# Asking for input loads five casts ahead instead of eight, in cast order, and putting fetches and stores ahead of them

## The chip, the core and the metric

The kernel runs on one core of a Trainium2 chip. The core has a matrix engine (TensorE, "PE" in the profile, with weight loads shown as "PEld"), three engines for elementwise work (VectorE or DVE, ScalarE or ACT, GpSimd or POOL), and SyncE (SP), which in this kernel only issues DMA transfers. Each engine works through its own instructions in the order in which they were written; they wait for one another with semaphores. The metric is the device time of one execution in microseconds (us).

## The reference

Two computations stand one behind the other. First causal attention over 8 batches, 8 heads, 576 tokens and head size 64, in which 16 "beacon" keys and values stand ahead of the sequence and are never masked. Its output, read as 4608 tokens of width 512, then goes through a feed-forward layer that takes the maximum of three products:

```python
k_all = concatenate([beacon_k, k], axis=2); v_all = concatenate([beacon_v, v], axis=2)
scores = scale * q @ k_all.T          # causal mask on the part behind the beacons
a = softmax(scores)
x = (a @ v_all) -> [4608, 512]
h = maximum(maximum(x @ w1, x @ w2), x @ w3)      # [4608, 768]
out = h @ w_out                                    # [4608, 512], float32
```

## The kernel before, in words

**Units of work.** Attention is done in pairs of heads: four pairs a batch, 32 pairs in all, numbered 0 to 31 (pair 20 is the first of batch 5). One step of the main loop (`emit_all`) belongs to each pair p from 8 on. A step emits, in this order: the scores of pair p (`emit_burst`, matmuls at L495, exponentials at L513); on every second step, the product with v for the two pairs before (`emit_pv_whole`, L615); the causal masks (L535, GpSimd); and several units of the feed-forward layer (L691 the three first products, L739 the last), which lag the attention by about a batch and fill TensorE. Finished outputs are called y and are stored to DRAM by SP (L771).

**How q and k reach TensorE.** Inputs come as float32. `load_pair` (L225) has SP load q and k of a pair into a stage buffer, `cast_pair` (L260) has GpSimd turn them into bf16. TensorE needs them transposed. For batches 0 to 3 TensorE transposes them itself (L387). For batches 4 to 7 (pair 16 on; `B_PE = 4`) three DMA steps do it: `store_pair` (L372) writes the bf16 pair to a DRAM buffer, and `fetch_pair` (L379 for q, L380 for k) reads it back through a transposing DMA into `qT` and `kT`, of which there are four each. In the plan, the fetch of pair p is asked for in step p-3, the store in step p-4, the cast in step p-5 (for pairs 16 to 18 at the end of that step). `open_dram` (L363) puts a batch's beacon keys into its DRAM buffer, in the step of the batch's first store.

**How v gets there.** `load_v` (L284, L289) loads the v of a batch in two pieces, written v b.0 and v b.1 here, and `cast_v` (L305) has GpSimd turn them into bf16 in step 4b+1. The product with v in step 4b+2 reads them first.

**Stage buffers and the list of loads.** All these loads go into one pool of eight stage buffers (`st_pool`). From batch 2 on they stand in a list `loads`, and `next_load` takes the next from it. `C(fn)` makes a planned cast ask for one load right behind it. So the number of loads asked for ahead of their casts is set once, at the point in `second_batch` where `next_load` is called for several at once (L980); after it each cast asks for one. In the kernel before the list runs batch by batch: four pairs, v b.0, v b.1.

**The order on SP.** Everything named above, apart from the weights and a few first loads, is issued by SP, one after the other. What a step asks for is kept in `plan` under (step, 0), which is run after the second feed-forward unit, and (step, 1), which is run at the end; within an entry it stands in the order in which `at_step` was called. A DMA that has to wait holds all that stand behind it in SP's queue: a load waits until the cast has freed its buffer, a store for its cast, a fetch for its store and for the scores that last read the same `qT`, a y for its copy out of PSUM. SP's DMAs also share eight completion semaphores in turn, so each waits, besides, for the landing of the one eight places before it.

Of the kernel before, what the change touches and what calls it, by code (L numbers as in the profile page):

```python
# [17 lines left out]
def kernel(  # L18
# [15 lines left out]
    B, H, S, D = q.shape  # L34
# [26 lines left out]
    PPB = H // 2  # L61
    PPQ = PPB // n_quad
    NPAIR = B * PPB
    RING = 4

    B_PE = 4
# [34 lines left out]
    def head(g, j):  # L101
        return 4 * g + j

    def place(p):
        b, pi = divmod(p, PPB)
        return b, pi // PPQ, 2 * (pi % PPQ)
# [98 lines left out]
    by_pool = nc.gpsimd.tensor_copy  # L205
# [8 lines left out]
    def new_stage(key):  # L214
        stage[key] = st_pool.tile([128, STW], FP32, name="st")
        return stage[key]

    def load_pair(p, gate=None):
        b, g, j0 = place(p)
        hs = slice(head(g, j0), head(g, j0) + 2)  # L220
        st = new_stage(("pair", p))
        if gate:
            gate.memset(st[0:QP, 0:1], 0.0)
        for i, src in enumerate((q, k)):
            nc.sync.dma_start(  # L225
                out=st[0:QP, i * NQ2 : (i + 1) * NQ2].rearrange("p (h x) -> p h x", h=2),
                in_=src[b, hs].rearrange("h (p r) d -> p h (r d)", r=QR),
            )
# [28 lines left out]
    def cast_piece(p, i, cast):  # L257
        st = stage["pair", p]
        t16 = pair_pool.tile([QP, QR, 2, D], BF16, name=f"p16{i}")
        cast(  # L260
            t16.rearrange("p r h d -> p h r d"),
            st[0:QP, i * NQ2 : (i + 1) * NQ2].rearrange("p (h r d) -> p h r d", h=2, r=QR),
        )
        stage["pair16", p, i] = t16
# [8 lines left out]
    def load_v(b, piece, gate=None):  # L273
        st = new_stage(("v", b, piece))
        if gate:
            gate.memset(st[:, 0:1], 0.0)
        t_lo, t_hi = V_PIECES[piece]
        for t in range(t_lo, t_hi):
            i = t - t_lo
            dst = st[:, i * H * D : (i + 1) * H * D].rearrange("p (h d) -> p h d", h=H)  # L280
            lo = 0
            if t == 0:
                lo = Nb
                nc.sync.dma_start(  # L284
                    out=dst[0:Nb], in_=beacon_v[b].rearrange("h n d -> n h d")
                )
            t0 = k_tok[t] + lo
            n = k_rows[t] - lo
            nc.sync.dma_start(  # L289
                out=dst[lo : lo + n], in_=v[b, :, t0 : t0 + n, :].rearrange("h p d -> p h d")  # L290
            )

    def cast_v(b, piece, cast):
        st = stage.pop(("v", b, piece))
        if b not in v_tiles:
            v_tiles[b] = v_pool.tile([128, n_kt, H, D], BF16, name="v_sb")
        v_sb = v_tiles[b]
        t_lo, t_hi = V_PIECES[piece]
        t = t_lo
        while t < t_hi:  # L300
            t1 = t + 1
            while t1 < t_hi and k_rows[t1] == k_rows[t]:
                t1 += 1
            n = k_rows[t]
            cast(  # L305
                v_sb[0:n, t:t1].rearrange("p t h d -> p (t h d)"),
                st[0:n, (t - t_lo) * H * D : (t1 - t_lo) * H * D],
            )
            t = t1
# [19 lines left out]
    def load_w_out():  # L329
        nc.gpsimd.dma_start(  # L330
            out=w_out_sb, in_=moe_w_out.rearrange("(t p) m -> p t m", p=128)
        )

    def load_beacons(b0, b1, dst, queue=None):
        for b in range(b0, b1):
            (queue or nc.sync).dma_start(
                out=dst[Nb * (b - b0) : Nb * (b - b0 + 1)],
                in_=beacon_k[b].rearrange("h n d -> n h d"),
            )
# [87 lines left out]
    def place_beacons(p, copy):  # L427
        b, pi = divmod(p, PPB)
        copy(kTs[p % NT][:, 0:Nb], bT[:, pi, Nb * b : Nb * (b + 1)])
# [74 lines left out]
    def emit_burst(p):  # L504
        at[p] = at_pool.tile([128, AT_W], BF16, name="at_sb")
        for gi, first in enumerate(next_pairs()):
            off = 0
            for t, q0, q1 in groups(p)[gi]:
                for e in range(2):
                    score(p, t, e, q0, q1, acc[:, first + e, off : off + q1 - q0])  # L510
                off += q1 - q0
            for e0, e1 in ((0, 1), (1, 2)) if gi == 0 else ((0, 2),):
                nc.scalar.activation(  # L513
                    out=both_heads(p, gi)[:, e0:e1],
                    in_=acc[:, first + e0 : first + e1, 0 : g_width(p, gi)],
                    func=AF.Exp,
                    scale=scale,
                )
# [3 lines left out]
    def emit_masks(p, gi, dve=False):  # L522
        masked.add((p, gi))
        off = 0
        for t, q0, q1 in groups(p)[gi]:
            n = k_rows[t]
            lo, hi = max(q0, k_tok[t]), min(q1, k_tok[t] + n)
            if lo < hi:
                view = both_heads(p, gi)[0:n, :, off + lo - q0 : off + hi - q0]
                x0 = lo - k_tok[t]  # L530
                if dve:
                    m = tri[0:n, None, x0 : x0 + hi - lo]
                    nc.vector.tensor_mul(view, view, m.to_broadcast([n, 2, hi - lo]))
                else:
                    nc.gpsimd.affine_select(  # L535
                        out=view,
                        in_=view,
                        compare_op=ALU.is_ge,
                        fill=0.0,
                        base=x0,  # L540
                        pattern=[[0, 2], [1, hi - lo]],
                        channel_multiplier=-1,
                    )
            off += q1 - q0
# [264 lines left out]
    def at_step(p, g, *fns):  # L809
        plan.setdefault((p, g), []).extend(fns)  # L810

    def L(fn, *a):
        return lambda: fn(*a)

    def load_pairs(p0, p1):
        return [partial(load_pair, p) for p in range(p0, p1)]

    loads = []
    def load_first_v(b):
        if b == B_PE - 1:  # L820
            load_beacons(B_PE, B, bk32)
        load_v(b, 0)

    for b in range(2, B):
        loads += load_pairs(b * PPB, (b + 1) * PPB) + [L(load_first_v, b), L(load_v, b, 1)]

    def next_load(n=1, **gate):
        for _ in range(n):
            if loads:
                loads.pop(0)(**gate)  # L830

    def C(fn, *a):
        def run():
            fn(*a)
            next_load()

        return run
# [40 lines left out]
    def F(n=1, new_ps=ffn_psum.tile):  # L878
        for _ in range(n):
            assert emit_ffn(END, new_ps)  # L880
# [88 lines left out]
    def second_batch():  # L969
        for p in range(PPB, 2 * PPB):  # L970
            place_beacons(p + 1, by_act)
            emit_burst(p)
            for gi in range(NG):
                emit_masks(p, gi)
                if p < PPB + 2 and 0 < gi < 3:
                    cast_piece(p + 2, gi - 1, by_pool)
                if p == 2 * PPB - 1 and gi == 1:
                    cast_v(1, 1, by_pool)
                    next_load(gate=nc.gpsimd)
                    next_load(6)  # L980
            if p < PPB + 2:
                stage.pop(("pair", p + 2))
            if p == PPB + 2:
                load_w_out()
                cast_v(1, 0, by_pool)
            if p + 1 < 2 * PPB:
                turn_pair(p + 1, by_dve)
                F(2, next_psum)
        F(4, next_psum)
        for p in range(2 * PPB, 2 * PPB + 2):  # L990
            cast_pair(p, by_pool, by_pool)
            next_load()
        finish = emit_pv_whole(n_quad)
        turn_pair(2 * PPB, by_dve)
        F(2, next_psum)
        finish()

    for p in range(2 * PPB + 2, B_PE * PPB):
        at_step(p - 2, 0, C(cast_pair, p, by_pool, by_pool))
    for b in range(2, B):  # L1000
        p = b * PPB
        at_step(p + 1, 0, C(cast_v, b, 0, by_pool))
        at_step(p + 1, 1, C(cast_v, b, 1, by_pool))
    at_step(B_PE * PPB - 5, 1, L(by_pool, bk16, bk32))
    for b in range(B_PE, B):
        p = b * PPB
        at_step(p - 4, 0, L(open_dram, b))
        for i in range(PPB):
            at_step(p + i - 5, int(p + i < 19), C(cast_pair, p + i, by_pool, by_pool))
            at_step(p + i - 4, 0, L(store_pair, p + i))  # L1010
            at_step(p + i - 3, 0, L(fetch_pair, p + i))


    def emit_all():
# [76 lines left out]
```

## Time and profile before

| what | value |
|---|---|
| median of 3 runs | 288.83 us (286.57 to 289.18) |
| profiled execution | 288.73 us, its span 287.0 us |
| TensorE busy | 275.5 us, 96% of the span |
| VectorE, ScalarE, GpSimd busy | 175.0, 159.5, 137.1 us |
| DMA | 50.59 MB, mean 176 GB/s; SP's queue 68.8% of 16 engines' span |
| granted TensorE clock | 0.998 of full speed |

The span is the time from the first to the last instruction of the profiled execution; the 1.7 us between it and the execution's time lie around it. The profile's views used below are: busy time by engine; busy time by stage (windows); waits, each with what ended it; the chain of work that ended last, followed back from the end; and the timeline of one engine, whose rows give start, duration, engine, line and tiles ("SPq" is SP's queue: the duration is that of the issue, not of the transfer). In the list of DMA issues the last two numbers are KB each and the median us from issue to landing.

### The profile page before, as it was taken

Reading aid. Unit: us, or ns where it says so; the run is one execution under the profiler, and the core shown is the slowest. Engines: PE = TensorE matmul, PEld = TensorE weight load, DVE = VectorE, ACT = ScalarE, POOL = GpSimd, SP = SyncE. Lnnn points to the kernel's source line nnn. Section 1 sums busy time; section 2 is a strip of 40 time slices with the busy share of each in tenths; the row PEclk is TensorE's granted clock in tenths of the full one; section 3 lists DMA queues with packets and bytes.
Section 4 is the critical chain, followed back from the end, with each engine's and each line's share of the span. In section 5 each row is a group of like instructions: output and inputs, shape, how many; then the busy total and the mean of one; then the engine's idle time right before and its main releaser. Section 6 shows DMA issues by size and latency. Waiting matters only on the chain.

```text
span 287.0 us, 7607 instructions
## 1 busy us (share of the span) xinstructions
PE 275.5 (96%) x2996; PEld 156.7 (55%) x2996; DVE 175.0 (61%) x303; ACT 159.5 (56%) x299; POOL 137.1 (48%) x282
## 2 busy tenths in 40 slices
PE   7889899999999999999998999899999999999995
PEld 3457674566555555555555787455555554444442
DVE  3784765773856757464735383538363847875773
ACT  3697595886668566756674858566675640000000
POOL 7271889567359955475544846284336210000000
PEclk9999999999999999999999999999999999999999
DMA  8999999999999999978999999848452003004004
GB/s 147 193 185 222 232 218 203 263 203 254 245 259 259 242 291 227 171 194 210 305 216 205 224 302 247 169 114 247 109 140 108 2 2 116 30 1 148 0 0 146
DMA packets 85315, 50.59 MB, mean 176 GB/s; under 512 B 64416, under 2 KB 80032, under 8 KB 85280
## 3 DMA queue, kind: packets, MB, share of 16 engines
q1 hardware_dynamic: 80672, 45.76, 68.8%
q0 software_dynamic: 4048, 4.03, 9.0%
q8 instruction: 23, 0.38, 0.6%
q10 hardware_dynamic: 560, 0.33, 0.5%
q14 instruction: 12, 0.10, 0.1%
HBM read 35.13 MB, written 14.22 MB: 172 GB/s over the span
## 4 chain that ended last, share of the span: by engine, by line
PE 79%; DMA 12%; POOL 3%; DVE 2%; issue 1%; ACT 1%; SPq 1%; POOLq 0%
PE acc L691 44%; PE acc L739 15%; PE acc L615 10%; PE acc L495 7%; DMA st<-in_v_dram 4%; DMA st<-in_k_dram 3%; DMA kT<-k_dram 2%; DMA quad<-in_k_dram 2%; PE acc L387 1%; POOL v_sb L305 1%; POOL at_sb L535 1%; ACT at_sb L489 1%; SPq L225 1%; DVE kT L415 1%; PE acc L757 0%
## 5 line engine op out<-in xcount | busy, mean ns | idle before, releaser
L691 PE MATMUL acc<-xT,w_sb 128*128 128x512 bf16 (+4 forms) x744 | 135.3, 338 | 0.0
L709 DVE TENSOR_TENSOR hT<-hT,acc 128x512 bf16<-128x512 bf16 x102 | 70.0, 688 | 59.1 <-PE acc L691 49.7
L691 PEld LDWEIGHTS <-w_sb 128*128 128x128 bf16 x744 | 69.3, 98 | 59.6
L535 POOL TENSOR_SCALAR_AFFINE_SELECT at_sb<-at_sb 128x256 bf16<-128x256 bf16 (+2 forms) x176 | 62.8, 378 | 75.1 <-ACT at_sb L513 71.1
L513 ACT ACTIVATE at_sb<-acc 128x208 bf16<-128x208 f32 (+3 forms) x140 | 89.5, 737 | 8.8 <-PE acc L495 7.5
L260 POOL CAST p<-st 96x768 bf16<-96x768 f32 x56 | 45.2, 831 | 10.2 <-DMA st<-in_q_dram 9.2
L739 PE MATMUL acc<-w_out_sb,hT 128*128 128x512 bf16 (+2 forms) x246 | 48.4, 348 | 0.0
L746 DVE COPY y<-acc 128x512 f32<-128x512 f32 (+1 forms) x35 | 21.9, 628 | 22.2 <-PE acc L739 13.3
L739 PEld LDWEIGHTS <-hT 128*128 128x128 bf16 x246 | 22.7, 98 | 21.8 <-DVE hT L709 1.6
L711 ACT CAST hT<-acc 128x352 bf16<-128x352 f32 x18 | 8.1, 452 | 47.0 <-PE acc L691 47.0
L711 DVE CAST hT<-acc 128x512 bf16<-128x512 f32 (+1 forms) x48 | 26.6, 554 | 9.1 <-PE acc L691 8.9
L495 PE MATMUL acc<-qT,kT 64*128 64x208 bf16 (+1 forms) x336 | 26.8, 280 | 3.6 <-DMA kT<-k_dram 2.9
L764 ACT COPY y<-acc 128x320 f32<-128x320 f32 x1 | 0.4, 425 | 46.0 <-PE acc L757 46.0
L495 PEld LDWEIGHTS <-kT 64*128 64x128 bf16 x336 | 15.4, 94 | 16.0 <-DMA kT<-k_dram 3.3
L638 DVE TENSOR_TENSOR xT<-raw,recip 128x576 bf16<-128x576 f32 x28 | 23.7, 887 | 0.0
L615 PE MATMUL acc<-at_sb,v_sb 128*32 128x512 bf16 (+5 forms) x672 | 22.8, 281 | 0.0
L625 ACT COPY raw<-acc 128x512 f32<-128x512 f32 x28 | 15.8, 633 | 4.8 <-PE acc L615 4.3
L305 POOL CAST v_sb<-st 128x1536 bf16<-128x1536 f32 (+2 forms) x21 | 18.2, 894 | 0.0
L615 PEld LDWEIGHTS <-v_sb 128*32 128x32 bf16 (+1 forms) x672 | 14.6, 96 | 6.7
L489 ACT ACTIVATE at_sb<-acc 128x1024 bf16<-128x1024 f32 (+3 forms) x16 | 13.1, 859 | 3.9 <-PE acc L480 3.8
L615 PE MATMUL acc<-at_sb,ones 128*32 128x512 bf16 (+3 forms) x336 | 14.9, 284 | 0.0
L433 DVE COPY kT<-acc 128x576 bf16<-128x576 bf16 x12 | 9.0, 753 | 6.4 <-PE acc L387 6.4
(69 smaller groups left out, 171.2 us busy)
## 6 DMA issues: line engine op xcount, KB each, us to landing
out_dram<-y SPq DMA_DIRECT2D x35, 256.0 KB, 3.4
st<-in_q_dram SPq DMA_DIRECT2D x28, 288.0 KB, 6.0
st<-in_k_dram SPq DMA_DIRECT2D x28, 288.0 KB, 6.6
st<-in_v_dram SPq DMA_DIRECT2D x24, 256.0 KB, 7.0
w_sb<-in_moe_w_dram POOLq DMA_DIRECT2D x6, 384.0 KB, 7.2
q_dram<-p SPq DMA_DIRECT2D x16, 144.0 KB, 2.8
k_dram<-p SPq DMA_DIRECT2D x16, 144.0 KB, 2.4
st<-in_v_dram SPq DMA_DIRECT2D x8, 224.0 KB, 7.0
```

Of the source, the lines that this page charges most:

```text
L260: cast(t16.rearrange("p r h d -> p h r d"), st[0:QP, i * NQ2 : (i + 1) * NQ2].rearrange("p (h r d) -> p h r d", h=2, r=QR),)
L305: cast(v_sb[0:n, t:t1].rearrange("p t h d -> p (t h d)"), st[0:n, (t - t_lo) * H * D : (t1 - t_lo) * H * D],)
L495: nc.tensor.matmul(ps, kTs[p % NT][hs, 128 * t : 128 * t + 128], qTs[p % NT][hs, q0:q1], start=True, stop=True, tile_position=(64 * e, 0),)
L513: nc.scalar.activation(out=both_heads(p, gi)[:, e0:e1], in_=acc[:, first + e0 : first + e1, 0 : g_width(p, gi)], func=AF.Exp, scale=scale,)
L535: nc.gpsimd.affine_select(out=view, in_=view, compare_op=ALU.is_ge, fill=0.0, base=x0, pattern=[[0, 2], [1, hi - lo]], channel_multiplier=-1,)
L615: nc.tensor.matmul(acc[32 * j : 32 * j + 32, bank, lo + q0 - qa : lo + qb - qa], lhsT, at_view(PPQ * quad + j // 2, t, j % 2, q0, qb), sta ...
L638: nc.vector.tensor_mul(xT[:, 2 * g + i, c0 : c0 + S], raw[:, i], recip)
L691: nc.tensor.matmul(ps[:, a:b], w_in[i][:, ct, 128 * ft : 128 * (ft + 1)], xT[:, ct, x0 : x0 + b - a], start=(ct == 0), stop=(ct == n_ct - 1),)
L709: nc.vector.tensor_max(h[:, lo:hi], h[:, lo:hi], ps[:, lo:hi])
L711: (by_act if hi < TOKB else by_dve)(h[:, lo:hi], ps[:, lo:hi])
L739: nc.tensor.matmul(ps[:, lo:hi], hT[:, ft, 128 * tt : 128 * (tt + 1)], w_out_sb[:, ft, lo:hi], start=(ft == 0), stop=(ft == n_ft - 1),)
L746: (by_act if hi < d_model else by_dve)(y[:, lo:hi], ps[:, lo:hi])
```

## The change

The list `loads` is sorted by the step in which each load is cast, in place of batch by batch; `cast_step` and `v_step` give that step and are now used for the casts as well. The burst in `second_batch` asks for three loads, not six. The planned entries of `open_dram`, `fetch_pair` and `store_pair` are written ahead of the casts (and so of the loads that the casts ask for), not among them; the fetch of a step comes ahead of its store. The beacon keys of batches 4 to 7 are loaded with pair 16, not with v 3.0.

```diff
-    def load_pairs(p0, p1):
-        return [partial(load_pair, p) for p in range(p0, p1)]
-
-    loads = []
-    def load_first_v(b):
-        if b == B_PE - 1:
+    def cast_step(p):
+        return (p - 2, 0) if p < B_PE * PPB else (p - 5, int(p < 19))
+
+    def v_step(b, piece):
+        return (b * PPB + 1, piece)
+
+    def load_turned_pair(p, **gate):
+        if p == B_PE * PPB:
             load_beacons(B_PE, B, bk32)
-        load_v(b, 0)
-
-    for b in range(2, B):
-        loads += load_pairs(b * PPB, (b + 1) * PPB) + [L(load_first_v, b), L(load_v, b, 1)]
+        load_pair(p, **gate)
+
+    loads = [(cast_step(p), 2 * (p >= B_PE * PPB), partial(load_turned_pair, p)) for p in range(2 * PPB, NPAIR)]
+    loads += [(v_step(b, i), 1, partial(load_v, b, i)) for b in range(2, B) for i in range(2)]
+    loads = [load for _, _, load in sorted(loads, key=lambda x: x[:2])]
...
                     next_load(gate=nc.gpsimd)
-                    next_load(6)
+                    next_load(3)
...
+    for p in range(B_PE * PPB, NPAIR):
+        if p % PPB == 0:
+            at_step(p - 4, 0, L(open_dram, p // PPB))
+        at_step(p - 3, 0, L(fetch_pair, p))
+        at_step(p - 4, 0, L(store_pair, p))
     for p in range(2 * PPB + 2, B_PE * PPB):
-        at_step(p - 2, 0, C(cast_pair, p, by_pool, by_pool))
+        at_step(*cast_step(p), C(cast_pair, p, by_pool, by_pool))
     for b in range(2, B):
-        p = b * PPB
-        at_step(p + 1, 0, C(cast_v, b, 0, by_pool))
-        at_step(p + 1, 1, C(cast_v, b, 1, by_pool))
+        for i in range(2):
+            at_step(*v_step(b, i), C(cast_v, b, i, by_pool))
     at_step(B_PE * PPB - 5, 1, L(by_pool, bk16, bk32))
-    for b in range(B_PE, B):
-        p = b * PPB
-        at_step(p - 4, 0, L(open_dram, b))
-        for i in range(PPB):
-            at_step(p + i - 5, int(p + i < 19), C(cast_pair, p + i, by_pool, by_pool))
-            at_step(p + i - 4, 0, L(store_pair, p + i))
-            at_step(p + i - 3, 0, L(fetch_pair, p + i))
+    for p in range(B_PE * PPB, NPAIR):
+        at_step(*cast_step(p), C(cast_pair, p, by_pool, by_pool))
```

The order of the two built programs on SP around the fetches of pairs 20 and 21, and of the loads from pair 12 on ("y" is a store of an output):

```
SP before: load 26, fetch 20, store 21, load 27, y, load v6.0, fetch 21, store 22, load v6.1, fetch 22
SP after:  y, fetch 20, store 21, load 25, load v5.0, y, load 26, fetch 21, store 22, load v5.1, fetch 22

loads before: 12 13 14 15 v3.0 v3.1 16 17 18 19 v4.0 v4.1 20 21 22 23 v5.0 v5.1 24 25 26 27 v6.0 v6.1 28 29 30 31 v7.0 v7.1
loads after:  12 13 16 14 17 15 v3.0 v3.1 18 19 20 21 v4.0 22 v4.1 23 24 25 v5.0 26 v5.1 27 28 29 v6.0 30 v6.1 31 v7.0 v7.1
```

The loads ahead of these (pairs 8 to 11, v 2.0, v 2.1) stand in the same order in both. The other four engines have the same instructions in the same order in both programs.

## The prediction

> **What bounds the kernel now.** I read the page's busy times first, then busy time by stage, then the waits of TensorE, then the chain of work that ended last, and at the end SP's own queue around the places that the chain names.
>
> ```profile
> span 287.0 us, 7607 instructions
> ## 1 busy us (share of the span) xinstructions
> PE 275.5 (96%) x2996; PEld 156.7 (55%) x2996; DVE 175.0 (61%) x303; ACT 159.5 (56%) x299; POOL 137.1 (48%) x282
> ```
>
> TensorE is busy for 275.5 of 287.0 us, so 11.5 us is all that it ever sits idle. A reordering that gives TensorE no less work can only win from these. Where they lie, by stage:
>
> ```profile
> core 0: us, PE busy (x) PEld busy (x) DVE busy (x) ACT busy (x) POOL busy (x), PEclk, DMA share, GB/s
> 60.00:148.00 88.00, 88.00 (x974) 48.84 (x971) 53.83 (x83) 61.28 (x120) 56.19 (x112) 1.00 1.04 240
> 148.00:153.00 5.00, 3.24 (x30) 1.93 (x29) 2.56 (x5) 1.75 (x5) 0.65 (x2) 1.00 0.97 178
> 153.00:180.00 27.00, 27.00 (x357) 20.62 (x355) 14.09 (x23) 18.23 (x33) 17.11 (x35) 1.00 1.15 243
> 180.00:183.00 3.00, 1.88 (x23) 1.21 (x21) 2.29 (x4) 0.82 (x3) 0.00 (x0) 1.00 0.78 183
> 183.00:240.00 57.00, 57.00 (x591) 30.27 (x588) 31.44 (x50) 35.13 (x65) 23.79 (x52) 1.00 0.39 103
> ```
>
> The first number after the stage's length is TensorE's busy time. From 60 to 240 us it is full except twice: 5.00 - 3.24 = 1.76 us idle around 150 us, and 3.00 - 1.88 = 1.12 us around 182 us. The remaining 8.6 us lie before 60 us and after 240 us, where the change reorders nothing that TensorE waits for (below). The last two columns matter as well: in the two long stages the DMA share is 1.04 and 1.15, so the DMA engines are fully booked at some 240 GB/s, and only after 183 us does the share fall to 0.39. The granted clock is 1.00 in all of them, so nothing here is a clock effect. What TensorE waited for at the two places:
>
> ```profile
> PE acc L495 <- DMA kT<-k_dram: 2.9, 2, 1.8
> ```
>
> Both times the first score matmul of a pair (L495) waited for the transposed k that `fetch_pair` brings. The chain of work shows which pairs:
>
> ```profile
> 113.48 0.85 PE acc L495 x11
> ...
> 142.56 0.85 PE acc L495 x11
> ...
> 149.08 2.73 DMA kT<-k_dram
> 151.81 0.05 issue
> 151.86 0.88 PE acc L495 x12
> ...
> 173.60 0.85 PE acc L495 x11
> ...
> 177.87 4.36 DMA kT<-k_dram
> ```
>
> Each step starts with its pair's L495 matmuls. Counted back from the last pair, 113.48 is pair 16, 142.56 pair 20, 151.86 pair 21 and 173.60 pair 24; the DMA at 149.08 is fetch 21, the one at 177.87 fetch 25. They are the second pairs of batches 5 and 6. Batch 4, without a stall, takes 142.56 - 113.48 = 29.08 us, or 7.27 us a step; batch 5 takes 173.60 - 142.56 = 31.04 us, 1.96 us more, of which 1.76 us are the idle time and 0.20 us a slower restart. Fetch 21 landed at 149.08 + 2.73 = 151.81 us; TensorE stood ready 1.76 us before 151.86, at 150.10. It was **1.7 us late**. Fetch 25 landed at 177.87 + 4.36 = 182.23 us, 1.1 us late.
>
> Why were they late? SP's queue just ahead of fetch 21:
>
> ```profile
> 142.08 0.40 SPq L771 DMA_DIRECT2D out_dram<-y  x1
> 142.58 0.38 SPq L284 DMA_DIRECT2D st<-in_beacon_v_dram  x1
> 143.01 3.88 SPq L289 DMA_DIRECT2D st<-in_v_dram  x3
> 146.98 2.06 SPq L379 DMA_TRANSPOSE qT<-q_dram  x1
> 149.08 1.26 SPq L380 DMA_TRANSPOSE kT<-k_dram  x1
> ...
> 151.54 1.14 SPq L289 DMA_DIRECT2D st<-in_v_dram  x2
> ```
>
> SP issues strictly in order. The three v DMAs of v 6.0 hold it for 3.88 us, 1.29 us each, against 0.57 us each for the two at 151.54: SP is held back by transfers in flight. Fetch 21 is requested by the program in step 18, before pair 19's burst, but SP reaches it in step 20 (146.98 lies behind 142.56). SP lags the program by two steps, because loads that nobody needs yet stand ahead of the fetch. How early those loads are:
>
> ```profile
> 186.78 1.46 POOL L305 CAST v_sb<-st 128x1536 bf16<-128x1536 f32 x1
> 188.18 1.59 POOL L260 CAST p<-st 96x768 bf16<-96x768 f32 x2
> 189.72 1.17 POOL L305 CAST v_sb<-st 128x512 bf16<-128x512 f32 x2
> ```
>
> These are the casts of v 6.0, of pair 30 and of v 6.1. The load issued at 143.01, whose back-pressure delayed the fetch, is first read at 186.78, over 40 us later.
>
> **The change part by part.** Only SP's queue changes: in the two built programs TensorE, VectorE, ScalarE and GpSimd have the same instructions in the same order. No byte and no DMA is added or removed.
>
> *Fewer loads ahead (the burst of six becomes three, so every later load is asked for about three casts later).* By the two orders on SP's queue, the loads that stood ahead of fetch 21 and now stand behind it are pair 27, v 5.1 and v 6.0. Ahead of fetch 25 they are pair 31, v 6.1 and v 7.0, the same sizes:
>
> ```profile
> st<-in_q_dram SPq DMA_DIRECT2D x28, 288.0 KB, 6.0
> ...
> st<-in_v_dram SPq DMA_DIRECT2D x24, 256.0 KB, 7.0
> ...
> st<-in_v_dram SPq DMA_DIRECT2D x8, 224.0 KB, 7.0
> st<-in_v_dram SPq DMA_DIRECT2D x8, 160.0 KB, 4.8
> ```
>
> A pair is q and k, 2 x 288 KB; v b.1 is 256 + 160 KB; v b.0 is 224 + 2 x 256 KB (and a small beacon part). Together 576 + 416 + 736 = 1728 KB, 1.77 MB, which at the 240 GB/s of the stage is 7.4 us of the DMA engines. If the queue stays full, fetch 21 lands 7.4 us earlier, 5.7 us before it is needed, and fetch 25 6.3 us before. If the queue does not stay full, SP has caught up with the program, and the fetches are earlier still, up to their place in the program. So the saving at the two places is bounded below by nothing (the lag does not shrink) and above by the whole stall; less than a quarter of the 7.4 us (1.7) removes the larger one, so I take the whole: 1.96 us for batch 5 and 1.12 us for batch 6, **3.08 us**.
>
> *Fetch and store ahead of the loads of the same step.* Fetch 20 no longer stands behind the load that the first v cast of step 17 asks for. But the second v cast's load, and with it three loads in all (25, v 5.0, 26), now lie between fetch 20 and fetch 21, where two lay (27, v 6.0). That is one pair, 576 KB or 2.5 us, more between these two, and it is already in the count of 1728 KB, which compares all that is ahead. I cost it at nothing beyond that; were it uncovered it would take 2.5 of the 5.7 us of slack.
>
> *Order of casts.* Pairs 16 and 17 are now loaded ahead of 14 and 15, as they are cast. GpSimd has waits there, but TensorE is at 88.00 of 88.00 us from 60 to 148, so no gain shows: nothing.
>
> *Loads no longer wait for the cast just before.* With three buffers more free, a load from pair 18 on finds its buffer free, and the stores now carry the wait for their cast themselves. Behind a waiting store stand the loads and fetches of the same step; the cast it waits for is a step older, so I take nothing; the bound is the lag itself (a rival below).
>
> *Before 60 us* the order on SP's queue is the same up to pair 12, so the idle time there stays; after 240 us only stores are left.
>
> **The sum** against the profiled execution: 288.73 - 1.96 - 1.12 = 285.65 us. What is late next is nothing on SP: TensorE is then full from 60 to 240 us, so no further gain can follow. The profiled 288.73 us stands 0.1 us under the median of 288.83 us, so the forecast is 1.1% below it; 1%, or 2.9 us, is about what a measurement of this kernel can tell from no change.
>
> **The rivals.** *One stall stays.* Three loads still stand ahead of fetch 21 and of fetch 25, and if SP's back-pressure, not the amount of work, sets the delay, one of the two may still be late: 288.73 - 1.96 = 286.8 or 288.73 - 1.12 = 287.6 us. For it speaks the 3.88 us that one v load holds SP; against it that v 5.0 now has a pair's load between it and the fetch. *The change does not do what it says:* the DMA engines, at a share above 1, keep the same lag, and the time stays at 288.7 us. Against it: work that is moved behind a fetch cannot delay it in an in-order queue.
>
> *Slower: the v loads come too late.* v 6.0 and v 6.1 are asked for four steps later than now (with the casts of steps 21 and 22, not 17 and 18), 29.08 us. At SP's present lag v 6.0 would be issued at 143.01 + 29.08 = 172.1 us, its last part 3.9 us later, and land 7.0 us after that, at 183.0, 3.8 us before its cast at 186.78. v 6.1 would go out at 151.54 + 29.08 = 180.6, and land 1.1 + 4.8 us later, at 186.5, 3.2 us before its cast at 189.72. Behind that cast there is no slack at all:
>
> ```profile
> 190.79 1.54 PE L615 MATMUL acc<-at_sb,v_sb 128*32 128x512 bf16 x40
> ```
>
> TensorE reads v_sb from 190.79, while the cast ends at 189.72 + 1.17 = 190.89. So if SP's lag *grew* by more than 3.2 us, TensorE would wait one for one, at v 4.1, v 5.1 and v 6.1, and the fetches would be later too. A growth of 4.2 us gives 288.73 + 3 x 1.0 = 291.7 us. Against it speaks that the lag should shrink by 7.4 us. The Trainium skill has a rule on this side: "DMA: Bandwidth & Descriptors", Rules for kernel authors, says to issue a DMA early and wait for it late. Applied to the loads it would give this rival's 291.7 us; applied to the fetches it speaks for the forecast. The trace has the loads over 40 us early and the fetch late, so I weigh it for the fetch.
>
> **How the numbers follow.** Forecast, both stalls gone: 0.70, 285.65 us, by its own range 285.3 to 286.0 (0.35 us, the distance between the upper two of the runs shown, 288.83 and 289.18). One stall stays: 0.15, 286.8 to 287.6. Nothing moves: 0.06, 288.7. v late: 0.09, about 291.7. The likeliest case gives 285.6. A range of 285.0 to 287.6 takes in the first two cases, with a little below for runs that come lower by themselves (one run before took 286.57), and leaves 0.15 out. Faster by over 1% means under 285.9 us: most of the first case, 0.55. Its remainder, 0.15, with one stall and with nothing moved make 0.36 within 1%. Slower: 0.09.
>
> **What would show it.** Right: TensorE at 88.00, 5.00, 27.00, 3.00 busy in the stages above (shifted), no wait of L495 for kT, a batch of 29.1 us for batches 5 and 6, SP reaching fetch 21 well before pair 20's burst, and v casts starting where they do now. One stall: one L495 wait left. Wrong on the slow side: GpSimd's L305 waiting for st<-in_v_dram, and TensorE's L615 for v_sb. The forecast also fails if the fetches are early but the span loses time before 60 us, where I hold the order to be the same.

## The result, and the profile after

| what | before | after |
|---|---|---|
| median of the runs | 289.0 us (286.57 to 289.98, 6 runs) | 285.32 us (284.76 to 286.7, 6 runs) |
| profiled execution | 288.73 us, span 287.0 us | 285.18 us, span 283.5 us |
| ratio after / before | | 0.9894, 95% interval 0.9849 to 0.9938 |

The changed kernel is 1.1% faster; the forecast was 285.6 us. Medians and ranges are of all runs of a kernel, while a ratio leaves out the runs in a slower state, over 1.5% longer than the kernel's fastest, and so is not the quotient of the medians. On another chip the same kernel took 285.31 us against 289.66 us (the run `after_again` below). The busy times on the page of the changed kernel:

```profile
span 283.5 us, 7622 instructions
## 1 busy us (share of the span) xinstructions
PE 274.7 (97%) x2996; PEld 156.4 (55%) x2996; DVE 172.7 (61%) x303; ACT 159.4 (56%) x299; POOL 136.4 (48%) x282
```

TensorE does the same work in a shorter span: idle time went from 11.5 to 8.8 us. Busy time by stage, with the columns as before (length, TensorE busy, then the other engines, granted clock, DMA share, GB/s):

```profile
60.00:148.00 88.00, 88.00 (x969) 48.63 (x967) 53.14 (x82) 61.21 (x118) 56.38 (x113) 1.00 1.06 240
148.00:153.00 5.00, 5.00 (x38) 2.77 (x37) 3.04 (x5) 3.64 (x6) 1.65 (x4) 1.00 1.06 231
153.00:180.00 27.00, 27.00 (x370) 21.00 (x368) 15.14 (x25) 17.21 (x35) 16.33 (x33) 1.00 1.15 230
180.00:183.00 3.00, 3.00 (x15) 1.36 (x14) 1.82 (x3) 2.26 (x3) 2.09 (x6) 1.00 1.24 210
183.00:240.00 57.00, 57.00 (x586) 30.23 (x585) 33.53 (x54) 32.29 (x61) 22.04 (x47) 1.00 0.47 117
```

Both holes are gone: 5.00 of 5.00 us and 3.00 of 3.00 us, and TensorE is full from 60 to 240 us. The DMA engines are booked as before up to 180 us; the two short stages that had a share of 0.97 and 0.78 now have 1.06 and 1.24. The chain of work that ended last, at the same pairs:

```profile
112.91 0.85 PE acc L495 x11
...
141.99 0.85 PE acc L495 x11
...
149.53 0.83 PE acc L495 x12
...
171.22 0.85 PE acc L495 x11
...
178.78 0.83 PE acc L495 x12
...
200.32 0.85 PE acc L495 x11
```

No DMA stands between them any more. Batch 4 takes 141.99 - 112.91 = 29.08 us, as before; batch 5 takes 171.22 - 141.99 = 29.23 us (31.04 before) and batch 6 takes 200.32 - 171.22 = 29.10 us (203.86 - 173.60 = 30.26 before, by the same view). So 1.81 + 1.16 = 2.97 us of the 3.55 us between the profiled executions are the two stalls. The other 0.57 us were there already at pair 20 (142.56 against 141.99), and all of them at pair 9 (59.78 against 59.20). SP's queue is the same in both programs up to 64 us, so the change did not bring them. The start differs from run to run: pair 8's burst comes at 52.5 to 57.2 us in the profiled executions of the kernels below. Now SP's queue ahead of fetch 21 and fetch 25:

```profile
136.65 0.43 SPq L225 DMA_DIRECT2D st<-in_q_dram  x1
137.13 0.47 SPq L225 DMA_DIRECT2D st<-in_k_dram  x1
137.70 1.16 SPq L379 DMA_TRANSPOSE qT<-q_dram  x1
138.90 1.26 SPq L380 DMA_TRANSPOSE kT<-k_dram  x1
...
166.91 2.02 SPq L379 DMA_TRANSPOSE qT<-q_dram  x1
168.97 1.26 SPq L380 DMA_TRANSPOSE kT<-k_dram  x1
...
171.37 1.21 SPq L289 DMA_DIRECT2D st<-in_v_dram  x2
```

SP reaches k of fetch 21 at 138.90, 3.1 us ahead of pair 20's burst (141.99); before it was 6.5 us behind it (149.08 and 142.56). The two transfers landed at 142.88 and 173.53 us, 6.65 and 5.25 us before the bursts that read them (149.53, 178.78).

Below, the time by which a fetch is early is the start of the burst that reads it minus its landing; where TensorE waits, it is late by that wait. Landings are the last completion of the transfer in the trace, and KB ahead of a fetch are the sizes of the loads issued from 20 us on and before it, added up.

### The profile page after: what moved, and what is told of

It reads as the page before. It is cut to its first block, busy times and chain, and to the rows that moved or that the text cites. A ratio compares the mean times of both kernels' runs of the same rounds, so it can differ in the third digit from the quotient of the medians.

```text
span 283.5 us, 7622 instructions
## 1 busy us (share of the span) xinstructions
PE 274.7 (97%) x2996; PEld 156.4 (55%) x2996; DVE 172.7 (61%) x303; ACT 159.4 (56%) x299; POOL 136.4 (48%) x282
## 4 chain that ended last, share of the span: by engine, by line
PE 82%; DVE 1%; issue 0%
PE acc L691 46%; PE acc L739 16%; PE acc L615 11%; PE acc L495 7%; PE acc L387 2%; PE acc L757 0%; DVE hT L709 0%; DVE qT L422 0%; DVE y L764 0%; DVE kT L433 0%
## 5 line engine op out<-in xcount | busy, mean ns | idle before, releaser
L495 PE MATMUL acc<-qT,kT 64*128 64x208 bf16 (+1 forms) x336 | 26.9, 280 | 1.1 <-DVE hT L730 0.6
L495 PEld LDWEIGHTS <-kT 64*128 64x128 bf16 x336 | 15.5, 94 | 13.3 <-issue 2.6
L615 PE MATMUL acc<-at_sb,v_sb 128*32 128x512 bf16 (+5 forms) x672 | 22.8, 281 | 0.0
L638 DVE TENSOR_TENSOR xT<-raw,recip 128x576 bf16<-128x576 f32 x28 | 21.8, 821 | 0.0
L615 PEld LDWEIGHTS <-v_sb 128*32 128x32 bf16 (+1 forms) x672 | 14.5, 96 | 6.7
L615 PE MATMUL acc<-at_sb,ones 128*32 128x512 bf16 (+3 forms) x336 | 14.9, 284 | 0.0
```

Source lines behind the costliest of these rows:

```text
L495: nc.tensor.matmul(ps, kTs[p % NT][hs, 128 * t : 128 * t + 128], qTs[p % NT][hs, q0:q1], start=True, stop=True, tile_position=(64 * e, 0),)
L615: nc.tensor.matmul(acc[32 * j : 32 * j + 32, bank, lo + q0 - qa : lo + qb - qa], lhsT, at_view(PPQ * quad + j // 2, t, j % 2, q0, qb), sta ...
L638: nc.vector.tensor_mul(xT[:, 2 * g + i, c0 : c0 + S], raw[:, i], recip)
```

## The experiments

Theory: SP's queue carries loads that nobody needs yet, and the fetches stand behind them; a smaller lead is the whole gain. Rivals: the order of the list, or the place of the fetches in the plan, brings it; or it is not SP's order but the bytes in flight. The table holds the readings that the sections below use.

| kernel | lead | list | fetches | ratio to before, 95% interval | wait of L495 for kT | fetch 25 |
|---|---|---|---|---|---|---|
| before | 8 | by batch | among casts | 1 | 2.9 us | 1.1 late |
| after | 5 | by cast | ahead | 0.9894 (0.9849 to 0.9938) | 0 | 5.25 early |
| after_again | 5 | by cast | ahead | 0.9849 (0.9799 to 0.9899) | 0 | 3.9 early |
| e2 | 5 | by batch | among casts | 0.9859 (0.9810 to 0.9908) | 0 | 2.4 early |
| e3 | 5 | by cast | among casts | 0.9834 (0.9783 to 0.9884) | 0 | 4.6 early |
| e13 | 8 | by cast | among casts | 1.0100 (1.0054 to 1.0147) | 6.3 us | 3.3 late |
| e5 | 8 | by batch | ahead | 1.0115 (1.0045 to 1.0185) | 5.5 us | 3.2 late |
| e1 | 8 | by cast | ahead | 1.0101 (1.0057 to 1.0145) | 4.2 us | 4.2 late |
| e8 | 7 | by cast | ahead | 0.9891 (0.9814 to 0.9969) | 2.2 us | 2.2 late |
| e10 | 6 | by cast | ahead | 0.9877 (0.9805 to 0.9949) | 0 | 0.75 early |
| e9 | 3 | by cast | ahead | 0.9887 (0.9826 to 0.9947) | 0 | 7.2 early |
| e4 | 2 | by cast | ahead | 1.0878 (1.0794 to 1.0962) | 0 | 16.4 early |
| e11, late v left out | 8 | by batch | among casts | 0.9898 (0.9851 to 0.9944) | 0 | 13.6 early |
| e12, late v from GpSimd | 8 | by batch | among casts | 1.0171 (1.0107 to 1.0235) | 5.5 us | 3.6 early |

### The change with the old lead (e1)

The changed kernel, with eight loads ahead.

```diff
-                    next_load(3)
+                    next_load(6)
```

> The changed kernel with the burst at six again (eight loads ahead); cast order and fetches ahead of the loads stay. Theory (work that stands ahead of a fetch on SP decides): 20320 KB of loads stand ahead of fetch 21 (20512 before, 18752 changed) and 24000 ahead of fetch 25 (24000 before, 22240 changed), so both waits of L495 for kT come back, about 0.9 us at pair 21 and 1.1 us at pair 25: 287.0 to 287.8 us. Rival (the new order, not the lead, removes the stalls): no wait for kT, 285.3 us.

Measured: 293.21 us (292.04 to 296.08, 10 runs) against 290.98 us, 1.0% slower than before. The waits of TensorE, and SP's queue ahead of fetch 25:

```profile
PE acc L495 <- DMA kT<-k_dram: 4.2, 1, 4.2
```

```profile
172.54 0.46 SPq L225 DMA_DIRECT2D st<-in_q_dram  x1
...
174.51 5.80 SPq L289 DMA_DIRECT2D st<-in_v_dram  x3
180.41 2.75 SPq L379 DMA_TRANSPOSE qT<-q_dram  x1
183.20 1.27 SPq L380 DMA_TRANSPOSE kT<-k_dram  x1
```

v 7.0 holds SP for 5.80 us, and k of fetch 25 goes out at 183.20, 14.2 us later than at a lead of five (168.97), though TensorE starts pair 24 only 3.8 us later (174.99 against 171.22). Fetch 21 was 2.2 us early, fetch 25 4.2 us late, where waits of 0.9 and 1.1 us had been expected. Without the smaller lead nothing of the gain is left. That it is *slower* than before, outside the 287.0 to 287.8 us expected, is more than a missing gain: the next runs take the edits apart.

### The smaller lead alone (e2)

The kernel before, with five loads ahead.

```diff
-                    next_load(6)
+                    next_load(3)
```

> The kernel before with the burst at three (five loads ahead); list batch by batch, fetches and stores among the loads as before. Theory: 18592 KB of loads ahead of fetch 21, 160 KB less than in the changed kernel, so no wait for kT in batches 5 and 6; but pair 16 is then asked for only one cast ahead of its own and pair 17 two, so GpSimd waits some 5 us for pair 16 near 80 us; where masks come late by that, TensorE loses between nothing and 3 us: 285.3 to 288.5 us, with any loss before 110 us. Rival (order, not lead): both waits for kT stay, 288.7 us.

Measured: 286.23 us (285.61 to 287.77) against 290.98 us. By stage:

```profile
148.00:153.00 5.00, 5.00 (x39) 2.76 (x37) 3.14 (x6) 3.58 (x7) 2.17 (x4) 1.00 0.78 197
153.00:180.00 27.00, 27.00 (x366) 20.93 (x366) 14.68 (x25) 17.22 (x34) 16.25 (x33) 1.00 1.02 221
180.00:183.00 3.00, 3.00 (x21) 1.42 (x18) 1.88 (x3) 2.92 (x5) 1.66 (x4) 1.00 0.72 159
```

Both holes close with one number changed. The order of the list and of the plan is not needed for the gain. It may add slack that TensorE has no use for: fetch 25 was 2.4 us early here, with 22,080 KB ahead of it, and 5.25 and 3.9 us early in the two profiles of the changed kernel, with 22,240 KB. The loss before 110 us that was held possible did not come.

### The two orders, one at a time, at both leads (e3, e5, e13)

e3 is the changed kernel with its fetches and stores among the casts, as before; e13 is e3 with a lead of eight; e5 is the kernel before with its fetches and stores ahead of the casts. The edit of e3:

```diff
-    for p in range(B_PE * PPB, NPAIR):
-        if p % PPB == 0:
-            at_step(p - 4, 0, L(open_dram, p // PPB))
-        at_step(p - 3, 0, L(fetch_pair, p))
-        at_step(p - 4, 0, L(store_pair, p))
...
-    for p in range(B_PE * PPB, NPAIR):
-        at_step(*cast_step(p), C(cast_pair, p, by_pool, by_pool))
+    for b in range(B_PE, B):
+        p = b * PPB
+        at_step(p - 4, 0, L(open_dram, b))
+        for i in range(PPB):
+            at_step(p + i - 5, int(p + i < 19), C(cast_pair, p + i, by_pool, by_pool))
+            at_step(p + i - 4, 0, L(store_pair, p + i))
+            at_step(p + i - 3, 0, L(fetch_pair, p + i))
```

> The changed kernel with the plan's fetches and stores among the casts again; list and lead of the change stay. Theory: the loads ahead of fetch 21 and fetch 25 are the same as in the changed kernel (18752 and 22240 KB), so no wait for kT and 285.3 us. Rival (it matters that a step's fetch stands ahead of the step's loads): 286.5 to 288 us with at least one wait for kT.

> The kernel before with the plan's fetches and stores ahead of the casts and their loads, nothing else: list batch by batch, eight ahead. Theory: loads ahead of fetch 21 and fetch 25 are as before (20512 and 24000 KB), both waits for kT stay, 288.7 us. Rival (fetches ahead of the loads of their step are the cure): 285.3 us.

> The changed kernel with the burst back at six (lead of eight) and with the planned fetches and stores among the casts as before: of the three edits only the order of the loads is left. With fetches and stores ahead of the loads and the sorted order, lead eight was 1.0% slower than before; fetches and stores ahead alone (batchwise order) 1.2% slower. If the plan's order is what harms at lead eight, this kernel stands at the kernel before, ratio 0.995 to 1.005, with fetch 25 about 1 us late. If the cast order harms too, it is at 1.005 to 1.01, with a wait of L495 for kT of over 2 us. If the cast order were a gain of its own, it would be under 0.995.

Measured: e3 285.75 us (284.77 to 287.31) and e5 295.2 us (291.83 to 296.75) against 290.98 us; e13 291.1 us (289.6 to 294.46, 10 runs) against 289.0 us. The waits of TensorE for kT, of e5 and of e13:

```profile
PE acc L495 <- DMA kT<-k_dram: 5.5, 2, 3.2
```

```profile
PE acc L495 <- DMA kT<-k_dram: 6.3, 4, 3.3
```

At a lead of five the plan's order makes no difference that can be seen (e3 and after). At a lead of eight either order alone is 1.0 to 1.2% slower than before, and so are both together. In e5 the first wait is for fetch 17: it landed 7.08 us after pair 16's burst before (120.56, 113.48), 0.5 us early, and 9.76 us after it here (122.47, 112.71), 2.2 us late. That is 2.7 us more. What stands ahead of fetch 17 in all is the same in both, 17,024 KB; but in e5 the loads of three pairs and v 5.0 stand between fetch 16 and fetch 17, before it was those of one pair and v 5.0, and v 5.0 held SP for 6.96 us, before for 4.86. Why two pairs' loads moved from ahead of fetch 16 to behind it delay fetch 17 is not shown. At a lead of five no delay of this kind reaches TensorE. Why each order costs about as much as both together stays open too: the KB asked for ahead of fetch 25 are the same 24,000 in e1, e5, e13 and before, so a count of all that stands ahead doesn't tell these four apart. The profiled executions of e1 and e13 (295.96 and 294.46 us) lie above the medians of their kernels, so a usual run may have shorter waits than these (in e1's, 3.4 us of the distance to before are there at pair 8 already, 57.15 against 53.74); that they are slower than before is read from the ratios.

### Leads between and below (e8, e10, e9)

The changed kernel with leads of seven, six and three.

```diff
-                    next_load(3)
+                    next_load(5)   # e8; next_load(4) in e10, next_load(1) in e9
```

> The changed kernel with the burst at five (seven loads ahead). Theory (KB of loads ahead of the fetch): 23232 KB ahead of fetch 25, between 22240 in the changed kernel, where it landed 5.25 us early, and 24000 with eight ahead, where it came 4.2 us late; in proportion it lands at about the time it is needed: a wait of 0 to 1 us, 285.5 to 287 us, no drop of the clock. Rival (only the eighth load, whose buffer is freed by the cast just before it, holds SP): fetch 25 is over 3 us early as in the changed kernel, 285.3 us.

> The changed kernel with the burst at four (six loads ahead). Theory: 22656 KB ahead of fetch 25, in proportion 3 us early, no wait for kT, 285.3 us like the changed kernel. Rival (the lead of five is special): over 287 us.

> The changed kernel with the burst at one (three loads ahead). The prediction's slower mechanism by itself: v 6.1 stands behind store 28 on SP, some 183 us, and lands some 2 us after the 186.2 us at which its cast starts in the changed kernel; likewise v 4.1 and v 5.1. GpSimd's L305 waits for st<-in_v_dram and TensorE for v_sb, one for one, about 2 us a batch: 288 to 292 us, fetches all early. Rival (loads have slack at three too): 285.3 us.

Measured, against 289.66 us: e8 287.13 us (285.41 to 290.38), e10 286.02 us (284.46 to 288.08), e9 286.21 us (285.15 to 286.84). Fetch 25 goes from 4.2 us late at a lead of eight to 2.2 late, 0.75 early, 5.25 early (3.9 in the second run) and 7.2 early at seven, six, five and three, and the wait ends between seven and six. This is the theory's own dose, in its direction but not in proportion to the KB: e8's wait is 2.2 us where 0 to 1 was expected, e10's slack 0.75 us where 3 was. The rival of e8, that only the eighth load holds SP, falls, since fetch 25 is late with seven. Below six a smaller lead gives fetches more slack and TensorE nothing, since it is full already. At three the v loads have used theirs up; the casts of v 6.1 on GpSimd in the changed kernel and in e9:

```profile
186.16 1.17 POOL L305 CAST v_sb<-st 128x512 bf16<-128x512 f32 x2
```

```profile
186.23 1.26 POOL L305 CAST v_sb<-st 128x512 bf16<-128x512 f32 x2
```

The 0.09 us more are a wait inside the group: v 6.1 landed at 186.82 us, between the two casts. In the changed kernel it landed at 177.55, 8.6 us before. The 288 to 292 us expected of e9 did not come: with less standing ahead of them, the v loads come just in time.

### One load less still (e4)

The changed kernel with a lead of two.

```diff
-                    next_load(3)
+                    next_load(0)
```

> The changed kernel with a lead of two: no burst, each cast asks for one load. This looks for the turning point of the slower rival. Lead three had v 6.1 landing just as its cast waited for it, with no time lost to speak of. Theory (one load less ahead puts each second v piece 7 us or so later than its cast can bear): GpSimd's L305 waits for st<-in_v_dram, TensorE's L615 waits for v_sb one for one, some us in each of batches 4 to 7, and after a long enough wait a lower granted clock: 295 us or more, GpSimd waits of 5 us and over. Rival (a smaller lead only shifts SP's queue, and the v loads stay in time because less stands ahead of them): 285 to 288 us.

Measured: 314.49 us (313.1 to 315.88, 2 runs) against 289.0 us. TensorE's and GpSimd's waits, and GpSimd's casts of v 6.1:

```profile
PE acc L615 <- POOL v_sb L305: 17.8, 10, 4.2
```

```profile
POOL v_sb L305 <- DMA st<-in_v_dram: 22.7, 11, 5.5
```

```profile
213.97 0.61 POOL L305 CAST v_sb<-st 128x512 bf16<-128x512 f32 x1 [4.54 <-DMA st<-in_v_dram]
215.03 0.61 POOL L305 CAST v_sb<-st 80x512 bf16<-80x512 f32 x1 [0.45 <-DMA st<-in_v_dram]
```

This is the slower rival of the prediction, by the waits that it named: GpSimd waits for v, and TensorE's L615 for GpSimd. They come at v 4.1, v 5.1 and v 6.1, as it said, and at v 2.1 and v 3.1 too. Its turning point lies between a lead of three and of two.

### Without the late v loads (e11)

The kernel before, lead of eight, with v of batches 4 to 7 neither loaded nor cast; the v of batch 3 stands in for it, so the outputs of these batches are not the reference's.

```diff
-        loads += load_pairs(b * PPB, (b + 1) * PPB) + [L(load_first_v, b), L(load_v, b, 1)]
+        loads += load_pairs(b * PPB, (b + 1) * PPB)
+        if b < B_PE:
+            loads += [L(load_first_v, b), L(load_v, b, 1)]
+        else:
+            loads += [lambda: None] * 2
...
+        if b < B_PE:
+            at_step(p + 1, 0, C(cast_v, b, 0, by_pool))
+            at_step(p + 1, 1, C(cast_v, b, 1, by_pool))
+        else:
+            at_step(p + 1, 0, next_load, lambda b=b: v_tiles.update({b: v_tiles[B_PE - 1]}))
+            at_step(p + 1, 1, next_load)
```

> The kernel before, lead of eight, but the loads and casts of v of batches 4 to 7 are left out, and the v of batch 3 is used in their place; every other DMA keeps its place on SP. So this kernel moves 4 x 1152 KB less. Theory (fetches 21 and 25 are late because SP's queue ahead of them is filled with early loads): without 5.1 and 6.0 ahead of fetch 21, and 6.1 and 7.0 ahead of fetch 25, both land in time; no L495 wait for kT from 60 to 240 us, 285.3 to 286 us on the terms of the profiled run of before (a ratio of 0.985 to 0.99). Rival (the transposing DMAs are slow by themselves, or the four qT and kT buffers set the time): the two waits stay at 1.76 and 1.12 us, ratio 1.00.

Measured: 285.72 us (285.68 to 287.44) against 289.0 us, a ratio of 0.9898 (0.9851 to 0.9944). By stage:

```profile
148.00:153.00 5.00, 5.00 (x38) 2.76 (x37) 3.14 (x6) 3.58 (x7) 2.17 (x4) 1.00 1.01 295
153.00:180.00 27.00, 26.95 (x366) 20.95 (x366) 14.68 (x25) 17.22 (x34) 13.80 (x30) 1.00 0.70 160
```

There is no wait for kT. Fetch 21 landed at 138.08 and fetch 25 at 165.81 us, 12.1 and 13.6 us before their bursts. Of the transposing DMAs and their buffers nothing was touched, so they are not the limit; the loads ahead of them are. Leaving these loads out frees their place on SP's queue and the DMA engines alike (the share from 153 to 180 us is 0.70, before 1.15); the next run tries to part the two.

### The v loads on another queue (e12)

The kernel before, with v of batches 4 to 7 issued by GpSimd.

```diff
+        queue = nc.gpsimd if b >= 4 else nc.sync
...
-                nc.sync.dma_start(
+                queue.dma_start(
```

> The kernel before, lead of eight, but the v loads of batches 4 to 7 are issued by GpSimd, not by SP, at the same place of the program; the same bytes move, as early as before. Theory A (the order and the hold on SP's queue delay the fetch: a v load of three DMAs held SP for 3.88 us): SP reaches fetch 21 several us earlier, no L495 wait for kT, a ratio of 0.985 to 0.99, if GpSimd's own casts don't come late from the issuing. Theory B (the bytes in flight on the DMA engines, booked over 1.0 from 153 to 180 us, delay it whatever the queue): fetch 21 and fetch 25 still land 1 to 2 us late, ratio 1.00.

Measured: 296.25 us (293.43 to 298.32) against 289.0 us, a ratio of 1.0171 (1.0107 to 1.0235). The chain of work (lines are one further down in this kernel, so L379 is L380), then TensorE's timeline at pair 24:

```profile
146.08 6.51 DMA kT<-k_dram
...
170.31 8.98 DMA kT<-k_dram
```

```profile
179.34 1.57 PE L496 MATMUL acc<-qT,kT 64*128 64x208 bf16 x12 [4.96 <-DMA kT<-k_dram]
```

The DMA at 146.08 is fetch 21. SP issued it 1.55 us after pair 20's burst (144.53); before it was 6.52 us after it. But it was under way for 6.51 us where it had taken 2.73, and so landed 8.06 instead of 9.25 us after that burst. Of the 5.0 us won on SP's queue, 3.8 were spent under way. Theory A, by which the hold on SP alone is the cause, falls: fetch 21 is still late by 0.5 us, and fetch 24, in time before, by 5.0 us. Theory B's numbers were not met either: fetch 25 was 3.6 us early, and the kernel is slower than before. The loads do not keep their times in this run. GpSimd issues v 6.1 at 138.73, ahead of fetch 21; on SP it had gone out at 151.54, behind it. And the wait at fetch 24 goes with where v 7.0 went, first on GpSimd here, then on SP in the kernel before:

```profile
162.08 2.62 POOL L290 DMA_DIRECT2D st<-in_v_dram  x3
```

```profile
166.64 1.14 SPq L379 DMA_TRANSPOSE qT<-q_dram  x1
...
172.30 0.38 SPq L284 DMA_DIRECT2D st<-in_beacon_v_dram  x1
```

SP's order had kept v 7.0 behind fetch 24 (166.64, then 172.30). GpSimd issues it at 162.08, and v 7.1 at 168.40, both ahead of fetch 24's k, which then took 8.98 us to land; it had taken 4.22. The 4.8 us more are close to the 5.1 us that these 1,184 KB take at 240 GB/s (an estimate from the stage's rate). So what counts is what is asked for ahead of a fetch, from whichever queue; how the delay at fetch 21 divides between SP's order and the bytes is not shown, as this run moves both. Part of the 1.7% is another cost: GpSimd issues these DMAs between its casts (2.62 us for three), and TensorE waited 1.7 us for v_sb in this kernel. The Trainium skill says as much, "DMA: Bandwidth & Descriptors", Rules for kernel authors: spreading DMAs over issuing engines does not help bandwidth, since all share the same 16 DMA engines. The trace agrees, by the 3.8 of 5.0 us at fetch 21 and the longer flight of fetch 24.

### The changed kernel again

No edit.

> The changed kernel itself, to stand beside the others on one chip. No wait of L495 for kT, granted clock 1.00 from 60 us to the end; 285 to 286 us where the kernel before takes 289 to 291.

Measured: 285.31 us (285.16 to 285.58) against 289.66 us (288.49 to 291.33), a ratio of 0.9849 (0.9799 to 0.9899).

## Why the prediction was right, step by step

- **The place of the gain** was right: the two waits of L495 for kT, and nothing else between 60 and 240 us. Forecast 1.96 + 1.12 = 3.08 us, measured 1.81 + 1.16 = 2.97 us. The time could not test more than that: any shift of the fetches by over 1.8 us takes both waits away.
- **The term that was mis-sized** is "0.20 us a slower restart". Batch 5 without a stall takes 29.23 us, 0.15 us more than batch 4. Most of the 0.20 belongs to the work of that batch, and batch 4 was not quite its measure.
- **1728 KB, 7.4 us earlier** held as a size. Against the burst of the pair before, fetch 21 landed 9.25 us after it and now 0.89 us after it, 8.4 us earlier; fetch 25 went from 8.63 to 2.31, 6.3 us earlier. The slack was forecast as 5.7 and 6.3 us and is 6.65 and 5.25 (5.5 and 3.9 in the second profile, where the fetches came 7.2 and 5.0 us earlier).
- **The reason, "SP is held back by transfers in flight"**, fits the traces, but no run tests it alone. The third v DMA of v 6.0 took 2.44 us to issue from 144.44 on; two DMAs into the same stage buffer had been issued ahead of it, and the DMA eight places before it had landed at 142.74, so neither the buffer nor the shared semaphores held it. e12 adds that the hold is not the whole delay. That early loads ahead of the fetch are the cause is shown by e2 (fewer of them) and e11 (none of v).
- **"I cost it at nothing"**, of the fetches ahead of the loads, holds only under the lead that the change has. At a lead of eight it costs 1.2% (e5). The price given, 2.5 us of slack at fetch 21 for one pair more, no run shows by itself: in e5 fetch 21 landed 7.4 us after the burst of the pair before it, 9.25 in the kernel before, but TensorE had lost 4 us at fetch 17 by then, which gives SP time; fetch 17 itself landed 2.7 us later, with two pairs more behind fetch 16.
- **"No gain shows: nothing"**, of the order of the casts, holds at a lead of five. At a lead of eight this order alone costs 1.0% (e13); the prediction had no price for that, and took the two orders as harmless by themselves.
- **One stall stays**: no run at a lead of five shows a wait for kT. At a lead of seven one does (e8).
- **The v loads too late**: the mechanism is real (e4) and the distance was given too small. At an unchanged lag v 6.1 had 3.2 us of slack; with the lag that shrank it has 8.6 (it landed at 177.55, not 186.5, while its cast came 3.6 us earlier), and v 4.1 and v 5.1 have 11.2 and 9.9. It takes two loads less to use that up and a third to lose time.
- **Before 60 us** the orders are the same, as it said, and 0.57 us of the result came from there all the same. That is a difference between runs, and luck that it went the way of the forecast.

## What to carry to other kernels

On a queue that is served in order, and on DMA engines that are booked full, a prefetch that goes out 40 us early is not free: it stands ahead of the transfer that is needed next, and moving it to another queue does not get it out of the way. Look at the transfer that is waited for, count what was asked for ahead of it and when that is first read, and shorten the lead until the wait goes; here six to three loads ahead do, eight are too many, seven left one wait, and two are too few. An order that costs nothing under a short lead may cost under a long one, so set the lead first.

## What the runs showed of the hardware beside this

A late fetch can cost more than its wait. TensorE's timeline in e8, e5 and e1 at a late burst (idle time before it in brackets), with the next step's burst, and under each the busy times of two short windows there, explained below:

```profile
181.93 0.88 PE L495 MATMUL acc<-qT,kT 64*128 64x208 bf16 x12 [2.18 <-DMA kT<-k_dram]
...
188.90 0.92 PE L495 MATMUL acc<-qT,kT 64*128 64x208 bf16 x12
```

```profile
177.71:181.12 3.41, 2.03 (x16) 1.17 (x14) 2.13 (x5) 0.88 (x2) 0.49 (x1) 1.00 1.33 126
181.12:184.53 3.41, 2.60 (x21) 1.35 (x22) 0.60 (x2) 2.25 (x5) 0.81 (x2) 1.00 1.25 269
```

```profile
122.52 0.88 PE L495 MATMUL acc<-qT,kT 64*128 64x208 bf16 x12 [2.27 <-DMA kT<-k_dram]
...
131.18 0.91 PE L495 MATMUL acc<-qT,kT 64*128 64x208 bf16 x12
```

```profile
120.16:123.57 3.41, 1.14 (x16) 0.62 (x15) 1.66 (x3) 0.85 (x4) 0.05 (x1) 1.00 1.03 133
123.58:126.98 3.40, 3.40 (x10) 1.16 (x9) 0.69 (x1) 2.49 (x3) 1.87 (x6) 0.50 1.19 212
```

```profile
186.73 1.57 PE L495 MATMUL acc<-qT,kT 64*128 64x208 bf16 x12 [4.18 <-DMA kT<-k_dram]
...
196.45 0.92 PE L495 MATMUL acc<-qT,kT 64*128 64x208 bf16 x12
```

```profile
182.19:185.60 3.41, 0.36 (x6) 0.16 (x3) 1.66 (x3) 0.44 (x1) 0.00 (x0) 1.00 1.23 115
185.61:192.43 6.82, 5.70 (x22) 2.21 (x23) 0.69 (x1) 3.20 (x5) 3.08 (x7) 0.50 0.91 199
```

After 2.18 us of idle time the step takes 188.90 - 181.93 = 6.97 us, its usual length. After 2.27 us it takes 8.66 us and after 4.18 us 9.72 us: the granted clock was 0.50 for 3.41 us from 123.58 in e5, and for 6.82 us from 185.61 in e1. So these two waits cost 1.7 and 2.75 us on top of themselves.

What decides is not the length of the gap alone. In all fourteen profiled executions the granted clock is 1.00 or 0.50, and the time between two of its changes is a whole multiple of 3.41 us (17 x 3.41 us in e5, from 126.99 to 185.01). This divides the span into slots of 3.41 us, in each of which the clock is constant; the windows above are one or two such slots each. The 2.27 us of e5 lie within one slot, 120.16 to 123.57. The 2.18 us of e8 are cut by a boundary at 181.12 us, which leaves 1.38 us idle in the slot before it and 0.81 in the one behind, and the clock stays at 1.00. From 20 us on, every slot at full clock in which TensorE was idle for 1.81 us or more was followed by half clock (15 slots, among them one of e4 whose longest single gap is 1.32 us), and none with 1.78 us or less was. So in these traces it is a slot more than half idle that halves the clock of the next one. Before 20 us this does not hold: two executions dropped after slots with 1.14 and 1.00 us idle. The Trainium skill, "TensorE: Matmul & The Clock Gate", Why this matters for your kernels, warns of idle gaps of over about 3 us; here 2.27 us within one slot were enough, and 2.18 us across two, 1.76 and 1.12 us were not.

It fits that e1, with 1.3 us more of waits than before, is slower by more than that (293.21 against 290.98 us): its ten runs had a mean clock of 0.982 to 0.994, those of before beside it 0.986 to 1.0. Early in the span, too, the clock differs between runs of one kernel: the second profile of the changed kernel has half clock from 15.70 to 19.11 us, the first none.
